# A two-part FFT and channel-mix kernel: engine order from a model in the program, and its PSUM as four bank pairs that any stage may take

## The chip, the core and the metric

The kernel runs on one core of a Trainium2 chip. The time is the device time in microseconds (us). The kernel before comes in two kinds: 802 to 806 us, with a mean granted clock of 0.932 to 0.938 where it is on record, and 810 to 816 us, mostly with 0.914 to 0.926 (four with 0.96). Its profiled execution took 815.3 us, so it is one of the slower kind, and a difference from its profile is up to 10 us larger than one from the faster kind. Runs of it over 1.5% above the fastest of their comparison (two near 815.5, and one at 2218.91) count as slow and are left out of the ratios. TensorE is the matmul engine (PE in the profile; PEld is its weight load), VectorE is DVE, ScalarE is ACT, GpSimd is POOL, and SP issues most DMAs.

## The reference

`x` is 8 batches of 3072 tokens by 256 channels. Cut to what matters:

```python
X = np.fft.rfft(x, axis=1)                     # along the tokens
Yr = Xr @ w_r - Xi @ w_i + b_r                 # complex mix of the channels
Yi = Xr @ w_i + Xi @ w_r + b_i
Y  = sign(Y) * maximum(abs(Y) - 0.01, 0)       # soft shrink of both parts
y  = np.fft.irfft(Y, n=3072, axis=1)
# channel mix: y_prev is y shifted by one token
xk = mu_k * y + (1 - mu_k) * y_prev
xr = mu_r * y + (1 - mu_r) * y_prev
k  = np.maximum(xk @ w_k, 0.0)                 # 256 -> 1024
v  = k * k @ w_v                               # 1024 -> 256
out = sigmoid(xr @ w_r) * v
```

## The kernel before

The transform of 3072 points is split into 96 x 32, so each batch passes through five kinds of units:

- **first**: 96-point transform, result A to SBUF (the on-chip memory), then to HBM (the chip's main memory) and back in another layout (A2);
- **middle**: second transform (XT), mix with the complex weights, the bias and the shrink (Y), and a first inverse step (V), which again goes to HBM and back;
- **last**: 96-point inverse transform (YT);
- **k, r, v**: the token part, in six tiles of 512 tokens per batch.

All matmuls of both kernels write to PSUM tiles. Their pools come to 4096 fp32 columns a kernel, counted here as 8 banks of 512. Before, these are bound to purposes: two single banks for transforms, two pairs for k, two single banks for r and v. In the start, before any token, transforms may use all of them.

```python
psF = ctx.enter_context(tc.tile_pool(name="psF", bufs=2, space=bass.MemoryType.PSUM))
psK = ctx.enter_context(tc.tile_pool(name="psK", bufs=2, space=bass.MemoryType.PSUM))
psV = ctx.enter_context(tc.tile_pool(name="psV", bufs=2, space=bass.MemoryType.PSUM))
# ...
def mix(u):
    ps = ps_fft()
    xt = XT.pop(u)
    for i in range(2):
        o = ps[:, 256 * i:256 * i + 256]
        g = 2 * u + i
        nc.tensor.matmul(o, bsel[:, 1 if g == 0 else 0, :], bb, start=True, stop=False)   # bias: 2 rows
        for w, z0, z00 in ((wr, 64, 128), (wi, 0, 0)):
            for c in range(NCD):
                # ...
                nc.tensor.matmul(o, lhs, w[:, c, :], start=False,
                                 stop=(w is wi and c == NCD - 1))
    r1 = r1_pool.tile([128, 512], BF16, name="r1")
    nc.scalar.activation(r1, ps, AF.Relu, bias=neglam, scale=1.0)
    # ... shrink on VectorE
# ... in last(b):
                eng = "act" if state["early"] and c else "dve"
                copy(eng, yt[:, c, :, half, 4 + 4 * qd:8 + 4 * qd, :],
                     ps[:, 0:384].rearrange("p (n h s) -> p h n s", n=4, h=3))
# ... the order in which the program is written:
        run(first(0))
        run(first(1))
        run(middle(0))
        run(last(0))
        state["early"] = False
        for b in range(B):
            # ... parts: middle(b + 1), first(b + 2), last(b + 1)
            merge(tokens(b), chain(*parts), 6 * 7.7, max(total, 1.0))
```

A scheduler then decides each engine's order from this program order and from what is free.

## Time and profile before

| | kernel before |
|---|---|
| median of the first runs | 805.62 us (804.62 to 813.5) |
| span of the profiled run | 813.5 us |
| TensorE busy | 694.5 us, 85% |
| VectorE, ScalarE busy | 540.5 us, 449.0 us |
| first token matmul | 117.3 us |
| from there to the last v matmul of the seventh batch | 629.2 us |
| from there to the last v matmul of the eighth | 61.3 us |
| from there to the end | 5.7 us |

The span runs from the first to the last instruction. The last four rows are read from the start times of the token matmuls in TensorE's timeline, and add up to it. I call them start, seven batches, last batch and tail. "Busy" counts an engine once while instructions overlap. Idle of TensorE, by who ended it (columns: total us, times, longest):

```profile
PE psK L386 <- DVE xk L374: 14.6, 24, 1.3
PE psF L265 <- DMA A<-Adr: 14.2, 1, 14.2
PE psF L341 <- DVE YT L226: 13.4, 34, 0.8
```

VectorE stands in two of the three: it copies the last transform and makes xk.

### The profile page before, as it was taken

What the parts mean: (1) busy time and instruction counts of PE and PEld (TensorE: products, weight loads), DVE (VectorE), ACT (ScalarE), POOL (GpSimd) and SP (SyncE); (2) the same over time, 40 slices, a digit from 0 to 9 for tenths busy, and PEclk for the clock granted to TensorE, in tenths of its full rate; (3) what the DMA queues carried; (4) which work ended last, traced back from release to release, by engine and by line L of the source; (5) the groups of instructions that cost most, each with busy time, mean ns of one, the idle gap of its engine ahead of it and who ended that gap; (6) DMA issues with size and microseconds to landing.
All of it is one profiled execution on the core that took longest, in us unless ns stands there. A gap on an engine that the chain in (4) does not pass through costs nothing.

```text
span 813.5 us, 12796 instructions
## 1 busy us (share of the span) xinstructions
PE 694.5 (85%) x4839; PEld 441.1 (54%) x4889; DVE 540.5 (66%) x1050; ACT 449.0 (55%) x661; POOL 24.7 (3%) x54
## 2 busy tenths in 40 slices
PE   2439659998999978998799978999799987998897
PEld 1125346665466635665366644666366653766565
DVE  6413249757966396765867587764967577775993
ACT  2324238683765735673566836675456736563463
POOL 5200000000000000000000000000000000000000
PEclk9655559999999989999899999999999999999799
DMA  9991131259222961347422881247413661135122
GB/s 162 233 223 41 52 79 26 67 144 258 52 52 72 234 162 27 91 114 205 110 65 66 214 201 27 64 100 226 110 47 85 193 144 27 52 95 139 27 78 78
DMA packets 75534, 90.38 MB, mean 111 GB/s; under 512 B 8912, under 2 KB 59856, under 8 KB 75472
## 3 DMA queue, kind: packets, MB, share of 16 engines
q1 hardware_dynamic: 69696, 75.53, 34.3%
q0 software_dynamic: 5776, 14.03, 9.8%
q8 instruction: 38, 0.62, 0.3%
q14 instruction: 24, 0.20, 0.1%
HBM read 53.22 MB, written 50.33 MB: 127 GB/s over the span
## 4 chain that ended last, share of the span: by engine, by line
PE 57%; DVE 17%; DMA 10%; ACT 7%; issue 3%; SPq 2%; another core or an unknown queue 0%; ACTq 0%; DVEq 0%
PE psV L419 14%; PE psK L386 12%; PE psF L292 11%; DVE YT L226 5%; PE psF L288 4%; DMA out_dram<-o 3%; PE psV L404 3%; ACT rl L390 3%; DVE k L395 3%; DVE xk L374 3%; PE psF L239 3%; PE psF L274 2%; DMA V<-Vdr 2%; PE psF L303 2%; PE psV L292 2%
## 5 line engine op out<-in xcount | busy, mean ns | idle before, releaser
L390 ACT ACTIVATE rl<-psK 128x1024 bf16<-128x1024 f32 x192 | 192.7, 1025 | 134.8 <-PE psK L386 129.7
L386 PE MATMUL psK<-xk,wk 128*128 128x512 bf16 x718 | 201.9, 398 | 23.7 <-DVE xk L374 14.6
L419 PE MATMUL psV<-wv,k 128*128 128x256 bf16 x1536 | 206.9, 273 | 1.4 <-ACT rg L408 1.2
L395 DVE TENSOR_TENSOR k<-rl 128x1024 bf16<-128x1024 bf16 x192 | 129.1, 687 | 73.5 <-ACT rl L390 73.5
L419 PEld LDWEIGHTS <-k 128*128 128x128 bf16 x1536 | 147.6, 98 | 35.1 <-issue 3.5
L386 PEld LDWEIGHTS <-wk 128*128 128x128 bf16 x768 | 76.2, 101 | 105.3 <-issue 37.0
L295 ACT ACTIVATE r<-psF,neglam 128x512 bf16<-128x512 f32 x86 | 59.2, 688 | 82.8 <-PE psF L292 82.4
L226 DVE CAST YT<-psF 128x384 bf16<-128x384 f32 x115 | 58.9, 552 | 37.8 <-PE psF L341 37.6
L292 PEld LDWEIGHTS <-XT 128*128 128x128 bf16 x768 | 62.2, 101 | 38.5 <-issue 14.2
L424 DVE TENSOR_TENSOR o<-psV,rg 128x512 f32<-128x512 f32 x96 | 65.5, 686 | 26.3 <-PE psV L419 24.0
L297 DVE SCALAR_TENSOR_TENSOR Y<-psF,r 128x512 bf16<-128x512 f32 x86 | 59.0, 686 | 33.5 <-ACT r L295 33.3
L224 ACT ACTIVATE XT<-psF 128x512 bf16<-128x512 f32 (+1 forms) x93 | 52.8, 581 | 40.6 <-PE psF L274 22.2
L408 ACT ACTIVATE rg<-psV 128x512 bf16<-128x512 f32 x96 | 56.4, 597 | 30.9 <-PE psV L404 30.4
L374 DVE SCALAR_TENSOR_TENSOR xk<-diff,muk,YT 128x512 bf16<-128x512 bf16 x96 | 68.5, 745 | 2.3 <-PE psK L386 1.8
L374 DVE SCALAR_TENSOR_TENSOR xr<-diff,mur,YT 128x512 bf16<-128x512 bf16 x96 | 67.8, 745 | 1.0 <-PE psV L404 0.7
L292 PE MATMUL psF<-wr,XT 128*128 128x256 bf16 x344 | 68.3, 281 | 0.0
L341 PE MATMUL psF<-FI,V 96*128 96x96 f16 x468 | 42.5, 219 | 29.4 <-DVE YT L226 13.4
L292 PE MATMUL psF<-wi,XT 128*128 128x256 bf16 x344 | 66.7, 276 | 0.0
L404 PE MATMUL psV<-wrm,xr 128*128 128x256 bf16 x384 | 58.7, 275 | 8.8 <-DVE o L424 7.0
L341 PEld LDWEIGHTS <-V 96*128 96x128 bf16 x512 | 35.4, 108 | 45.5 <-issue 29.1
L224 ACT ACTIVATE A<-psF 96x512 bf16<-96x512 f32 x101 | 55.3, 603 | 3.0 <-DMA Adr<-A 2.1
L288 PE MATMUL psF<-bb,bsel 2*128 2x256 bf16 x172 | 47.9, 279 | 5.1 <-ACT XT L224 3.9
(115 smaller groups left out, 522.9 us busy)
## 6 DMA issues: line engine op xcount, KB each, us to landing
out_dram<-o SPq DMA_DIRECT2D x192, 128.0 KB, 2.2
xs<-in_x_dram POOLq DMA_DIRECT2D x32, 384.0 KB, 8.6
Adr<-A SPq DMA_DIRECT2D x32, 384.0 KB, 8.0
A<-Adr SPq DMA_DIRECT2D x32, 384.0 KB, 6.4
Vdr<-V SPq DMA_DIRECT2D x192, 64.0 KB, 1.8
V<-Vdr SPq DMA_DIRECT2D x32, 384.0 KB, 7.0
wk<-in_moe_w_k_dram POOLq DMA_DIRECT2D x1, 512.0 KB, 9.1
wv<-in_moe_w_v_dram POOLq DMA_DIRECT2D x1, 512.0 KB, 8.7
```

What stands on the lines that cost most here:

```text
L224: nc.scalar.activation(out, in_, AF.Copy, bias=0.0, scale=1.0)
L226: nc.vector.tensor_copy(out=out, in_=in_)
L288: nc.tensor.matmul(o, bsel[:, 1 if g == 0 else 0, :], bb, start=True, stop=False)
L292: nc.tensor.matmul(o, lhs, w[:, c, :], start=False, stop=(w is wi and c == NCD - 1))
L341: nc.tensor.matmul(ps[:, 96 * i:96 * i + 96], V2[b, n2 // 8][:, n2 % 8, 128 * c:128 * c + 128], FI, start=True, stop=True)
L374: nc.vector.scalar_tensor_tensor(out=m[:, c, :], in0=diff[:, c, :], scalar=mu[:, c:c + 1], in1=yp[:, c, :], op0=ALU.mult, op1=ALU.add)
L386: nc.tensor.matmul(ps[:, 512 * f:512 * f + 512], wk[:, c, 128 * ff:128 * ff + 128], xk[:, c, :], start=(c == 0), stop=(c == NCD - 1))
L390: nc.scalar.activation(rl, ps, AF.Relu, bias=0.0, scale=1.0)
L395: nc.vector.tensor_tensor(out=K2[t][:, 2 * i:2 * i + 2, :].rearrange("p f n -> p (f n)"), in0=rl, in1=rl, op=ALU.mult)
L404: nc.tensor.matmul(ps[:, 256 * i:256 * i + 256], xr[:, c, 128 * q:128 * q + 128], wrm[:, c, :], start=(c == 0), stop=(c == NCD - 1))
L419: nc.tensor.matmul(ps[:, 256 * i:256 * i + 256], K2[t][:, ff, 128 * q:128 * q + 128], wv[:, ff, :], start=(ff == 0), stop=(ff == NCF - 1))
L424: nc.vector.tensor_tensor(out=o[:, 2 * p:2 * p + 2, :].rearrange("p q d -> p (q d)"), in0=ps, in1=RG.pop((t, p)), op=ALU.mult)
```

## The change

The intent: keep TensorE fed all the time. The program no longer leaves the order to the scheduler. It simulates the engines while it is being written out: it picks, of six streams of units, the ready one that is due first, gives it whichever bank pair comes free first, lets the engine that would end sooner do each copy, and writes the instructions out in that order. Units are two banks wide. The bias is padded to 128 rows. Loads at the start are reordered. The diff, cut to its core:

```diff
+    ctx.enter_context(tc.manual_schedule())
-    psF = ctx.enter_context(tc.tile_pool(name="psF", bufs=2, space=bass.MemoryType.PSUM))
-    psK = ctx.enter_context(tc.tile_pool(name="psK", bufs=2, space=bass.MemoryType.PSUM))
-    psV = ctx.enter_context(tc.tile_pool(name="psV", bufs=2, space=bass.MemoryType.PSUM))
+    psum = ctx.enter_context(tc.tile_pool(name="psum", bufs=1, space=bass.MemoryType.PSUM))
+    banks = psum.tile([128, 4, 1024], FP32, name="banks")
 ... pools: XT 4 to 3, r1 3 to 2, Y 4 to 3, V 2 to 3, V2 5 to 4, rg 5 to 3 (some of twice the size)
-    bb = const.tile([2, D], BF16, name="bb")
+    bb = const.tile([128, 2, D], BF16, name="bb")
+    nc.vector.memset(bb, 0.0)
 ...
+    def run_on(eng, ready, us):
+        free[eng] = max(ready, free[eng]) + us
+        return free[eng] + 0.1
+    def cheaper(ready, act_us, dve_us):
+        a, d = max(ready, free["act"]) + act_us, max(ready, free["dve"]) + dve_us
+        return "act" if a <= d else "dve"
+    def take():
+        f, i = min((f, i) for i, f in enumerate(pair_free) if f is not None)
+        pair_free[i] = None
+        return banks[:, i, :], i
 ... each stage rewritten as units with a due time, a TensorE time and a list of needs
+                if u or half:
+                    nc.tensor.matmul(ps[:, base:base + 512], bsel[:, 0, :], bb.rearrange("p a d -> p (a d)"),
+                                     start=True, stop=False)
 ... after A2 of batch 0 has been asked for:
+                        nc.gpsimd.tensor_copy(out=junk, in_=A2[0][:, 0, 0:1])
+                        load_big()
+                        for n in range(4):
+                            load_x(1, n)
 ...
+    P = 74.0
+    START = 60.0
+        fb += first(b, 0.0, 1.0) if b == 0 else first(b, *((45.0, 52.0) if b == 1 else (s - 0.9 * P, s - 0.1 * P)))
+        fa += middle(b, 20.0, 44.0) if b == 0 else middle(b, s, s + 0.5 * P)
+        fc += last(b, 55.0, 60.0) if b == 0 else last(b, s + 0.75 * P, s + 0.95 * P)
 ...
+    while any(n < len(s) for n, s in zip(place, streams)):
+        flush(t)
 ...     of the streams' next units that are ready, issue the one due first
```

## The prediction

> **What bounds the kernel now.** I read the page's summary first, then busy time by stretches of the run, then the chain of waits around one slow stretch, then TensorE's timeline instruction by instruction.
>
> ```profile
> PE 694.5 (85%) x4839; PEld 441.1 (54%) x4889; DVE 540.5 (66%) x1050; ACT 449.0 (55%) x661; POOL 24.7 (3%) x54
> ...
> PEclk9655559999999989999899999999999999999799
> ```
>
> TensorE looks busy for 85% of the span, but matmuls overlap, so this isn't time at full rate. The clock row shows about half speed from 40 to 130 us. I therefore count streaming time. In the TensorE timeline ten back-to-back 256-column matmuls take 1.25 us with the last at 0.27, so one needs (1.25 - 0.27)/9 = 0.109 us. A 512-column one needs 0.215, a 128-column one 0.056 and a 96-column one 0.043 (same method). Per batch of the eight: k 96 x 0.215 = 20.7; v 192 x 0.109 = 20.9; r 48 x 0.109 = 5.2; together 46.9 for the token part. Middle: second transform 2.7, bias 24 x 0.109 = 2.6, mix 96 x 0.109 = 10.5, back 24 x 0.109 = 2.6, sum 18.4. First 16 x 0.215 = 3.4; last 64 x 0.043 = 2.7. In all 71.4 us per batch. The boundary between batches (the wait for V) recurs at 271, 363, 456, 548, 640 and 733 us: a period of 92.4 us. So 21 us per period are not streaming.
>
> Where they are lost, by stretches (columns: stretch, its length, busy us and count of each engine, clock, DMA share, GB/s):
>
> ```profile
> 37.00:53.00 16.00, 1.12 (x3) 0.29 (x3) 2.57 (x4) 2.15 (x4) 0.51 (x1) 0.50 1.12 258
> 53.00:98.00 45.00, 41.73 (x192) 21.98 (x190) 14.30 (x30) 18.09 (x31) 0.00 (x0) 0.50 0.28 63
> 98.00:108.00 10.00, 0.00 (x0) 0.00 (x0) 0.00 (x0) 0.00 (x0) 0.00 (x0) 0.50 0.67 176
> ...
> 283.00:315.00 32.00, 23.66 (x153) 12.26 (x156) 25.67 (x56) 13.27 (x16) 0.00 (x0) 0.89 0.45 121
> 315.00:350.00 35.00, 33.67 (x268) 22.89 (x268) 25.37 (x46) 21.55 (x35) 0.00 (x0) 1.00 0.29 76
> ```
>
> First loss: the stretch 283 to 315, where the last transform meets the first tokens of the next batch. Adding up the streaming time of the matmuls that start in it gives 17.6 of 32 us: 14 us lost. The chain of waits there is VectorE alone:
>
> ```profile
> 287.00 3.40 DVE YT L226 x7
> 290.40 0.60 DVE diff L369
> 291.00 0.47 DVE YT L226
> 291.47 1.33 DVE xk L374 x2
> ```
>
> All the copies of the last transform go to VectorE, while ScalarE is at 13.27 of 32 us. Second loss: the bias matmuls, which use 2 of 128 rows. TensorE's timeline:
>
> ```profile
> 333.25 0.38 PE L292 MATMUL psF<-wi,XT 128*128 128x256 bf16 x2
> 333.56 0.28 PE L288 MATMUL psF<-bb,bsel 2*128 2x256 bf16 x1
> 333.77 0.39 PE L292 MATMUL psF<-wr,XT 128*128 128x256 bf16 x2
> ```
>
> Two wi matmuls need 0.22 from 333.25, so the bias could start at 333.47. It starts 0.09 late, and what follows starts 0.21 later instead of 0.11. One bias matmul costs about 0.20 us beyond its own streaming; 24 per batch are 4.8 us. That leaves 21 - 14 - 4.8 = about 2 us per period for all else. Third loss: the start. The first token matmul runs at 117.3 us.
>
> [...] VectorE takes 0.552 for 384 columns and 0.688 for 512, so 1.06 ns a column and 0.14 fixed; ScalarE takes 0.598 for 512 and 1.025 for 1024, so 0.17 fixed. [...] Here TensorE is 41.73 of 45 us busy from 53 to 98 and stays at 0.50, so I can't count on a release at a given point.
>
> **The change part by part.**
> 1. Bias rows padded to 128 (zeros) and, but for the first pair of each batch, one 512-column matmul for two of 256. Streaming stays 2.6 us per batch; the switching goes: -4.8 us per batch, on the path wherever TensorE is the bound. Seven batches after the start: -34.
> 2. Two-bank units. For VectorE, 96 gatings and 96 shrinks of 0.69 become 48 + 48 of an estimated 0.144 + 1024 x 0.00106 = 1.23, which saves 96 x 0.14 = 13 us. ScalarE: 96 mix relus and 96 gates become 48 + 48, saving 96 x 0.17 = 16. Mostly beside TensorE; worth something only in the boundary.
> 3. Copies chosen by who would end first. From the built order of instructions, ScalarE gets 49 of 64 A copies, 51 of 64 YT, 33 of 48 V and 38 of 48 wide XT. ScalarE's sum: 192 x 1.0 + 48 x 1.03 + 48 x 1.1 + 120 x 1.03 + 51 x 0.85 = 462. VectorE's: squares 132, xk and xr 136, diff 33, gating and shrink 118, copies 66, negations and pads 27 = 512. Per batch about 58 and 64 against 71.4 of TensorE: no new bound, but not much slack (80 to 90%).
> 4. Emission in the order of the model, units chosen by readiness, any of four bank pairs. Before, the last transform's 16 units had two one-bank buffers and ran back to back. Now it is due at 75 to 95% of the previous period, interleaved with tokens, and V is asked for half a period earlier. I expect 4 of the 14 us to remain, plus 2 for stalls of an order fixed in advance.
> Period: 71.4 + 4 + 2 = 77.4 us.
> 5. The start. x of batch 0 alone loads first; batch 1's x and the three large weights wait until A2 has arrived; batch 1's first transform follows the middle. Before, DMA was full from 0 to 53 us and A2 (issued at 37.0) landed at 52.9. Now 1.57 MB of x and 0.26 of wr and wi at the measured 161 GB/s are in at about 13 us; A stores of 7 to 8 us end near 24, and A2 [...] lands near 32. The middle took 45 us at half clock; without the switching (24 x 0.2[...]) and with wider units I take 33. Then 10 for the round trip of V and 3 for the last units: tokens from about 78 us, against 117.
>
> Sum: 78 + 7 x 77.4 + last batch. Tokens alone stream 46.9; before, the last stretch took 60 us, 51 of them TensorE busy, with TensorE waiting on VectorE. I take 50. Gating and storing at the end: about 4. 78 + 542 + 50 + 4 = 674, taken as 670: the last two batches have no first transform, which takes off up to 2 x 3.4.
>
> **The rivals.**
> A. TensorE becomes almost continuous and the start gets the full clock. For it: after the bias has gone, only about 2 us per period of other loss were left, and ready work is chosen from six streams. Period 74.5, tokens at 70: 70 + 521 + 49 + 4 = 644.
> B. A fixed order that does not fit. Engines now run in a sequence derived from constants; where a DMA or a wait comes later than assumed, an engine stands before an instruction whose data isn't there while later ones are ready. A mix or v unit holds a bank pair for about 5 us (2.2 or 3.5 of matmuls plus 1.2 to 2.4 of reading), so two of them leave two pairs. Evidence: V took 12.1 us to arrive on the chain at 271 us, more than the 7 us that the diff assumes. Against: the read is now asked for well ahead. Period 84, tokens at 85: 85 + 588 + 52 + 4 = 729.
> C. VectorE becomes the bound. At 64 of 77 us it isn't on average, but squares, token mixing and shrink come in bursts. Period 80 to 82: about 700.
> D. Slower or unchanged: needs a period near 92 again. Only a wrong dependency across the shared bank tile would do that. The built waits of TensorE name single later points of ScalarE and VectorE and do not follow every instruction, so I think it unlikely.
>
> **Range and chances.** Half weight on the main sum, a quarter each side of it; B at its full size is a tail. Predicted 670 us, 636 to 712 eight times in ten. Being within 2% would need more than 110 us to go wrong: faster 0.95, within 2% 0.03, slower 0.02.
>
> **What would show it.** Step 1: no idle before bias weight loads, where the waits before had 43.3 us in 176 cases. Step 3: VectorE near 512 us busy, ScalarE near 462. Step 4: the wait for V off the chain, periods of 75 to 80 us, no stretch of 30 us with half of TensorE's streaming. Step 5: first token matmul before 85 us. I am wrong if the period exceeds 84, if the start stays over 90 us, or if waits on bank pairs or of VectorE lead the chain throughout.

In step 5 two terms go: how the arrival of A2 was counted, and what the delays around the two-row matmuls were taken to be at half clock. The 32 and the 33 us there still count them, so the sum is as recorded: 78 + 542 + 50 + 4 = 674, taken as 670. Without the two, A2 (1.57 MB at the 230 GB/s of 20 to 40 us, so 7 us) lands at 24 + 7 = 31, and the first middle takes 45 - 24 x 0.2 = 40.2 less what the wider units save. "The switching" is the 0.20 us that a bias matmul costs beyond its own streaming. The clock is at half from 27.4 to 119.6 us of the trace, and the DMA share from 0 to 53 us is 1.01.

## The result

The changed kernel takes 667.56 us (median of 4 runs, 664.56 to 670.45); the kernel before took 809.56 in the same comparison. The ratio is 0.8243 (95% interval 0.816 to 0.8326). A ratio is the mean time of one kernel's fast runs over that of the other's of the same rounds, so it is not quite the ratio of the two medians.

| | before | after | difference |
|---|---|---|---|
| start | 117.3 | 87.3 | -30.0 |
| seven batches | 629.2 | 524.4 | -104.8 |
| last batch | 61.3 | 44.8 | -16.5 |
| tail | 5.7 | 6.3 | +0.6 |
| span | 813.5 | 662.8 | -150.7 |

The spans differ by more than the medians (142.0 us), because the profiled execution of the kernel before is one of its slower kind and that of the changed kernel is the fastest of its four. The last batch of the kernel before begins at 746.5 us and still holds matmuls of the last transform until 760.4 us; in the changed kernel they are over before it begins. So not all of the 16.5 us there is a gain of the token part.

The page of the changed kernel, same lines as in the prediction:

```profile
PE 593.6 (90%) x4722; PEld 435.5 (66%) x4801; DVE 483.8 (73%) x732; ACT 443.5 (67%) x469; POOL 25.2 (4%) x57
...
PEclk9689579999999999999999999999999999999999
```

TensorE has lost 94 to 101 us of busy time although it streams almost the same columns (593.6 us here with 79 matmul records missing, 600.2 in the control with none missing): a part was half clock in the start (27.4 to 119.6 us before, 23.1 to 36.7 and 64.0 to 84.5 now), a part the delay around the two-row matmuls (96 ns before one and 101 ns after it, the medians at full clock in the kernel before). How much each was isn't worked out here. After the start the clock stays high: its mean from 87 to 662 us is 0.99, and it is at half only from 91.3 to 98.2 and from 313.2 to 316.6. The dips of the kernel before at each boundary of batches, 3.4 to 10.2 us each, have gone.

By stretches:

```profile
32.00:56.00 24.00, 20.87 (x176) 16.69 (x180) 14.36 (x17) 12.41 (x13) 5.19 (x9) 0.90 0.91 173
56.00:87.00 31.00, 14.78 (x100) 9.29 (x99) 12.15 (x17) 13.62 (x17) 4.04 (x8) 0.67 0.99 238
...
247.00:323.00 76.00, 72.11 (x576) 53.01 (x585) 58.56 (x86) 52.08 (x56) 2.03 (x4) 0.98 0.59 143
```

The first line is the first middle stage: 24 us, where the kernel before needed 45 at half clock. The second is the round trip of V: TensorE is idle half of it, and the DMA share is 0.99. The third is one ordinary period of 76 us: TensorE 72 us busy, VectorE 58.6, ScalarE 52.1. After the start no stretch of 30 us streams for less than 23.8 us (added up matmul by matmul in the control's trace).

The bias in TensorE's timeline:

```profile
49.75 0.60 PE L418 MATMUL banks<-Y,GI 128*128 128x256 bf16 x4
50.19 0.38 PE L383 MATMUL banks<-bb,bsel 128*128 128x512 bf16 x1
50.40 0.38 PE L394 MATMUL banks<-wr,XT 128*128 128x256 bf16 x2
```

Four matmuls of 0.109 from 49.75 end at 50.19, where the bias starts; it streams 512 columns in 0.21 and the next starts at 50.40. Nothing is lost on either side any more.

What TensorE waits for now:

```profile
PE banks L344 <- DMA A<-Adr: 23.5, 5, 12.4
PE banks L287 <- ACT A L234: 11.7, 1, 11.7
PE banks L287 <- DMA xs<-in_x_dram: 7.0, 2, 6.0
PE banks L489 <- DMA V<-Vdr: 3.6, 4, 1.6
```

Waits for VectorE have left the head of this list. In their place stands the DMA of A2 (the first line): once 12.4 us in the start, and then (23.5 - 12.4)/4 = 2.8 us on average before the middle of a batch can begin. The chain of waits shows how the two transfers follow each other ahead of one of these middles:

```profile
217.17 8.52 DMA Adr<-A
227.27 8.81 DMA A<-Adr
```

Store, wait, load: from 217.2 to 236.1 us is 18.9 us, where the model in the program counts 5 + 7.

### The profile page after: what moved, and what is told of

It is laid out like the page before. It is cut to its first block, busy times and chain, and to the rows that moved or that the text cites. A ratio compares the mean times of both kernels' runs of the same rounds, so it can differ in the third digit from the quotient of the medians.

```text
span 662.8 us, 12033 instructions
## 1 busy us (share of the span) xinstructions
PE 593.6 (90%) x4722; PEld 435.5 (66%) x4801; DVE 483.8 (73%) x732; ACT 443.5 (67%) x469; POOL 25.2 (4%) x57
## 3 DMA queue, kind: packets, MB, share of 16 engines
q0 software_dynamic: 5840, 14.03, 12.5%
## 4 chain that ended last, share of the span: by engine, by line
PE 66%; DMA 17%; ACT 6%; DVE 5%; issue 3%; SPq 1%; POOL 0%; DVEq 0%; ACTq 0%; POOLq 0%
PE banks L617 22%; PE banks L575 19%; PE banks L394 11%; DMA Adr<-A 7%; DMA A<-Adr 6%; PE banks L600 4%; ACT rl L581 3%; PE banks L361 3%; PE banks L418 2%; PE banks L383 2%; ACT A L234 2%; PE banks L287 2%; DMA Vdr<-V 1%; DVE V L236 1%; PE banks L489 1%
## 5 line engine op out<-in xcount | busy, mean ns | idle before, releaser
L581 ACT ACTIVATE rl<-banks 128x1024 bf16<-128x1024 f32 x192 | 195.0, 1029 | 86.1 <-PE banks L575 73.2
L575 PE MATMUL banks<-xk,wk 128*128 128x512 bf16 x706 | 191.1, 383 | 4.0 <-DVE xk L553 1.4
L617 PE MATMUL banks<-wv,k 128*128 128x256 bf16 x1536 | 184.5, 274 | 0.4 <-DVE k L587 0.3
L402 ACT ACTIVATE r<-banks,neglam 128x1024 bf16<-128x1024 f32 x48 | 53.4, 1113 | 40.6 <-PE banks L394 39.4
L406 DVE SCALAR_TENSOR_TENSOR Y<-banks,r 128x1024 bf16<-128x1024 f32 x48 | 58.5, 1222 | 28.1 <-ACT r L402 28.0
L394 PE MATMUL banks<-wr,XT 128*128 128x256 bf16 x384 | 73.8, 274 | 0.9
L394 PE MATMUL banks<-wi,XT 128*128 128x256 bf16 x384 | 73.8, 274 | 0.0
L624 DVE TENSOR_TENSOR o<-banks,rg 128x1024 f32<-128x1024 f32 x48 | 58.5, 1218 | 7.7 <-PE banks L617 7.7
L234 ACT ACTIVATE XT<-banks 128x1024 bf16<-128x1024 f32 (+2 forms) x39 | 37.8, 970 | 35.4 <-PE banks L361 23.5
L234 ACT ACTIVATE A<-banks 96x1024 bf16<-96x1024 f32 x49 | 49.2, 1020 | 17.6 <-DMA Adr<-A 12.0
L600 PE MATMUL banks<-wrm,xr 128*128 128x256 bf16 x384 | 49.8, 272 | 3.5 <-ACT rl L581 2.2
L600 PEld LDWEIGHTS <-xr 128*128 128x128 bf16 x384 | 37.1, 97 | 14.1 <-issue 3.8
```

The lines of the kernel that those rows point to most:

```text
L234: nc.scalar.activation(out, in_, AF.Copy, bias=0.0, scale=1.0)
L394: nc.tensor.matmul(o, lhs, w[:, c, :], start=False, stop=(w is wi and c == NCD - 1 and (i == 1 or not (u or half))))
L406: nc.vector.scalar_tensor_tensor(out=y, in0=ps, scalar=LAM, in1=r1, op0=ALU.add, op1=ALU.min)
L575: nc.tensor.matmul(ps[:, 512 * f:512 * f + 512], wk[:, c, 128 * ff:128 * ff + 128], xk[:, c, :], start=(c == 0), stop=(c == NCD - 1))
L581: nc.scalar.activation(rl, ps, AF.Relu, bias=0.0, scale=1.0)
L600: nc.tensor.matmul(ps[:, 256 * q:256 * q + 256], xr[:, c, 128 * q:128 * q + 128], wrm[:, c, :], start=(c == 0), stop=(c == NCD - 1))
```

## The experiments

Twelve kernels ran, all with correct results. They ran in four rounds, each on another chip: the control, two-row bias, halves and fixed engines; then single pairs, scheduler's order, early loads and the padded old kernel; then the earlier first transform, both mends and three parts undone; then two and two. The control ran in the first round alone. The kernel before had medians of 812.23 to 813.89 in the four, so a difference of 2 us between rounds says nothing. "Start", "seven batches" and so on are those of the profiled run.

### The changed kernel again (control)

> The changed kernel unchanged, as the control for the runs beside it. Both theories: 664 to 671 us, ratio to the kernel before 0.82 to 0.83, first token matmul near 87 us, period of the middle batches near 76 us.

667.83 us (666.72 to 668.91), ratio 0.823. Start 90.1, seven batches 523.9, last 44.8. This is the number that the others are compared with; the start moves by some 3 us from run to run.

### Bias back to two rows

```diff
-                    nc.tensor.matmul(ps[:, base:base + 512], bsel[:, 0, :], bb.rearrange("p a d -> p (a d)"),
+                    nc.tensor.matmul(ps[:, base:base + 512], bsel[0:2, 0, :], bb[0:2].rearrange("p a d -> p (a d)"),
-                        nc.tensor.matmul(o, bsel[:, 1 - i, :], bb[:, 0, :], start=True, stop=False)
+                        nc.tensor.matmul(o, bsel[0:2, 1 - i, :], bb[0:2, 0, :], start=True, stop=False)
```

> The changed kernel with the bias rows cut back to 2 of 128 (still one 512-column matmul where the change has one). 13 bias matmuls a batch remain 2-row. Theory 1 (each change between a 2-row and a 128-row matmul costs TensorE 0.1 us on each side, and TensorE is the bound): 8 x 13 x 0.20 = +21 us, 685 to 692 us, and the idle before bias weight loads comes back (about 0.2 us in some 100 cases). Rival (TensorE has slack that takes it up): under +6 us. Besides: if the 2-row matmuls were what held the clock at a half in the first middle stage of the kernel before, the stretch from 32 to 56 us stays at half clock here and the first token matmul moves from 87 us to about 97; if not, it stays within 3 us of 87.

683.67 us (679.89 to 687.43), ratio 0.8425: +16 us. In the profiled run, the slowest of the four, the seven batches took 543.2 (+19) and the start 91.4 (+1). The weight loads of the bias wait again:

```profile
PEld L383 <- issue: 21.8, 69, 0.4
PEld L394 <- issue: 20.4, 88, 0.3
```

The first line is the bias, the second the mix weights right after it, which in the changed kernel waited 0.8 us in all.

From start to start in the trace, the median delay is 95 ns before a 2-row matmul and 101 ns after it, the same for 512 columns as for 256. So theory 1 holds: 0.2 us per bias matmul, on TensorE's path, though the median lies 1 us under its range. The second question got the answer no: the recorded clock was full from 35.4 us to the end of that stage, much as in the control (from 36.6), and its mean over 32 to 56 us is 1.00 (0.90 in the changed kernel), so 13 two-row matmuls did not hold the clock down here. In the changed kernel, then, the padding is not what gives the start its clock.

### The kernel before with the bias padded, nothing else

```diff
-    bb = const.tile([2, D], BF16, name="bb")
+    bb = const.tile([128, D], BF16, name="bb")
+    nc.vector.memset(bb, 0.0)
 ... bsel likewise; its two rows are written as before
```

> The kernel before with nothing but the bias rows padded to 128 with zeros (still two 256-column matmuls). Theory 1 (0.20 us saved per bias matmul, 192 of them, where TensorE is the bound): ratio to the kernel before 0.94 to 0.97, that is -25 to -45 us, the idle of 43 us before bias weight loads gone, and perhaps more if the first middle stage then gets the full clock (another -10 to -20). Rival (the time saved turns into waits for VectorE and for banks): ratio over 0.98.

769.29 us against 813.89, ratio 0.9496: -44 us by the medians, and about -35 against the faster kind of the kernel before (802.39 to 804.6 in this round). Against the profiled execution, one of the slower kind, it falls in two parts. Seven batches went from 629.2 to 603.4 (-25.8), and the idle of 43.3 us before the bias weight loads has gone. The start went from 117.3 to 97.6 (-19.7), nearly all of it in the first middle stage. About 6 us of that are the delays around the two-row matmuls: at half clock their medians in the kernel before were 140 and 109 ns, and 24 x 0.25 = 6.0. The rest goes with the clock:

```profile
53.00:98.00 45.00, 29.02 (x266) 24.46 (x267) 20.89 (x53) 22.08 (x42) 0.00 (x0) 0.75 0.46 111
```

In the kernel before this stretch has a clock of 0.50 and TensorE is busy 41.73 us. Here the recorded clock is full from 58.5 us and returns to half only at 79.0, after the stage is over. Nothing but the padding differs, and the four runs with it agree (767.86 to 769.55), so in these profiles the half clock went with the 24 two-row matmuls of that stage. It need not do so in every execution: the faster runs of the kernel before (802 to 806 us) have the same 24 and a higher mean clock, and none of them was profiled. With the run before this: 24 went with the half clock, 13 did not, though the width and order of the units differ between the two as well. What decides it isn't shown.

### Two-bank readings cut into one-bank halves

```diff
-                    nc.scalar.activation(r1, ps, AF.Relu, bias=neglam, scale=1.0)
+                    for z in (slice(0, 512), slice(512, 1024)):
+                        nc.scalar.activation(r1[:, z], ps[:, z], AF.Relu, bias=neglam, scale=1.0)
 ... likewise the shrink, the gate, the gating, and the two halves of each copy
```

> The changed kernel, same bank pairs and nearly the same order, but every reading of a bank pair is done in two one-bank halves (the relu and shrink of the mix, the gate, the gating, and the copies; the relu of k stays whole, as in both kernels). About 267 more ScalarE instructions and 156 more VectorE ones. Theory 1 (wide readings save ScalarE and VectorE time that is mostly off TensorE's path): ScalarE busy +30 to +40 us, VectorE +15 to +20, time +0 to +10 us. Rival (VectorE or ScalarE is the bound): +20 us or more.

662.36 us (660.18 to 664.64), ratio 0.8163: 5 us faster than the control, whose four runs lie between 666.72 and 668.91. ScalarE's busy time rose from 443.8 to 466.6 (+23) and VectorE's from 484.2 to 494.1 (+10), less than expected, because instructions that follow each other overlap (their durations added up rose by 55 and 23). In the profiled run 2 us of the gain lie in the start, 2 in the seven batches and 0.5 in the tail. So wide readings are no gain in this kernel; they cost about 0.8%. Neither theory said that. A reading of one bank is shorter (0.598 us against 1.025 for two on ScalarE in the kernel before), so the first bank of a halved unit could come free sooner for the next matmuls; whether it does, and whether that is the cause, no run here isolates.

### Engines of the copies fixed

```diff
-    def copy(ready, out, in_, act_us, dve_us):
-        eng = cheaper(ready, act_us, dve_us)
+    def copy(ready, out, in_, act_us, dve_us, eng="act"):
 ... YT copies get "dve", V copies "dve" if u % 2 else "act"
```

> The changed kernel with each copy's engine fixed as in the steady part of the kernel before: A and XT on ScalarE, V by turns, YT on VectorE. VectorE gets about 51 more YT copies of 0.95 us and loses some 25 others. Theory 1 (the boundary between batches was lost to VectorE's copies of the last transform, and the free choice of engine is what mended it): +10 to +25 us, with VectorE waits of the last transform's matmuls back on the chain. Rival (interleaving the last transform with tokens mends it by itself, whichever engine copies): under +5 us.

682.21 us (681.22 to 684.11), ratio 0.841: +14 us, of which 6 in the start (96.2) and 10 in the seven batches (533.7). The size fits theory 1, but its sign of recognition failed: no wait of the last transform for VectorE is among TensorE's larger waits; the DMAs of A2 (26.1 us) and V (14.1 us) lead. The free choice of engine is worth 14 us; that it is worth them at the boundary isn't shown. Ten us in seven batches are 1.4 of the 14 us per period that the prediction put down to these copies.

### Order left to the scheduler

```diff
-    ctx.enter_context(tc.manual_schedule())
```

> The changed kernel without the manual schedule: the same program, pairs and engine choices, but each engine's order is left to the scheduler that orders the kernel before. Theory 1 (the order made by the model is a large part of the gain): +25 us or more, with waits of TensorE between batches. Rival (bank pairs, wide units, bias and the engine choice make the gain, and the program's order is good enough for any scheduler): within 10 us of the changed kernel.

691.27 us (690.13 to 694.84), ratio 0.8544: +23 us, 19 of them in the seven batches (542.9), 6 in the start. That is just under theory 1's 25 and far from the rival's 10. Its sign, waits of TensorE between batches, is weak: nine waits for V, 9.9 us in all. The order that the model gives is worth about 23 us. The program is still written in the model's sequence here, so this is the value of holding to it exactly, not of the model as a whole.

### Three parts undone at once

The last, the fixed engines and the two-row bias together.

> The changed kernel with three parts undone at once: bias rows of 2, engines of the copies fixed, and the order left to the scheduler. Alone these cost 16, 14 and 24 us. If they are independent: 668 + 54 = 722 us, and the remaining 90 us up to the kernel before lie in what is left: the units taken by readiness from six streams into freely shared bank pairs, and the start. If they cover for one another (each lets the others' lost time show): 740 us or more.

730.4 us (729.72 to 733.07), ratio 0.9029. Alone the three cost 16, 14 and 23, together 53; at once they cost 63. That is 10 us more than the sum, and halfway between the two expectations (722 and 740), so they cover for one another a little. What remains to the kernel before, 82 us by the medians (812.23 and 730.4), lies in parts that none of the three touches. No wait of the last transform for VectorE leads TensorE's list here either; the DMA of V does (23.2 us).

### One pair for all transforms

```diff
+    PAIRS = {0: (0, 1), 1: (2,), 2: (3,), 3: (3,), 4: (3,), 5: (0, 1, 2, 3)}
-        f, i = min((f, i) for i, f in enumerate(pair_free) if f is not None)
+        f, i = min((pair_free[i], i) for i in PAIRS[s] if pair_free[i] is not None)
 ... stream 0 is k and r, 1 is v, 2 middle, 3 first, 4 last, 5 the tables; slot_ready(s) likewise
```

> The changed kernel with the four bank pairs bound to stages: two for k and r, one for v, one for all transforms and the mix (nearest to the kernel before in two-bank units); the order is made anew by the same model. Theory 1 (free use of pairs is part of the gain: with one pair a transform's matmuls wait for the reading of the one before): a mix unit holds its pair for some 5 us and a transform for some 1.7, so a batch's middle, first and last need 6 x 5 + 28 x 1.7 = 78 us of one pair, which is over the period of 76: period 80 to 95, time +30 to +120 us. Rival (pairs have slack; only the order matters): under +10 us.

893.14 us (890.72 to 897.39), ratio 1.1034: slower than the kernel before. Periods were about 102 us. TensorE stands before its own stage's single pair:

```profile
PE banks L289 <- ACT A L234: 49.0, 44, 1.2
PE banks L491 <- ACT YT L234: 38.6, 43, 0.9
```

Each of these is a matmul that waits for the reading of the unit before it, some 0.9 to 1.1 us at a time. The clock suffers too: its mean is 0.837 against 0.961 in the control, with 34 us at half clock in a period (209.6 to 243.7 us, and again from 312.0). How much of the 225 us is the clock and how much the waits isn't separated. The kernel before had two single banks for the same units. With the due times left as they were, units two banks wide in a single pair lose the whole gain and more.

### Two pairs for tokens, two for the rest

```diff
+    PAIRS = {0: (0, 1), 1: (0, 1), 2: (2, 3), 3: (2, 3), 4: (2, 3), 5: (0, 1, 2, 3)}
```

> The changed kernel with the bank pairs bound more mildly than in the run with single pairs: two for the token stages (k, r, v), two for the transforms and the mix; order made anew by the same model. By holding times a token part needs 24 x 2.1 + 6 x 2.1 + 6 x 4.9 = 92 us of two pairs per batch, 46 of a period of 76, and the rest 78 us of two pairs, 39 of 76. Theory 1 (free sharing itself is a large part of the gain, since each side at times needs three pairs or more): +15 to +60 us, and the last batch, tokens alone on two pairs, goes from 44.8 us to 50 or more. Rival (only a stage left with a single pair is slow, as that first run was; two and two are as good as four shared): under +8 us, last batch within 2 us of 44.8.

720.14 us (714.23 to 724.18), ratio 0.8861: +52 us. Start 101.5, seven batches 553.7, last batch 55.6. The last batch is the clean case, tokens with nothing else beside them. TensorE there, with two pairs:

```profile
685.62 1.03 PE L577 MATMUL banks<-xk,wk 128*128 128x512 bf16 x4
687.76 1.03 PE L602 MATMUL banks<-wrm,xr 128*128 128x256 bf16 x8 [1.11 <-ACT rl L583]
688.63 1.03 PE L577 MATMUL banks<-xk,wk 128*128 128x512 bf16 x4
689.90 1.91 PE L619 MATMUL banks<-wv,k 128*128 128x256 bf16 x16 [0.25 <-ACT rg L607]
```

My reading is that a v unit sits on one pair, so k and r take turns on the other and wait for ScalarE. TensorE is idle for 8.3 of 56 us in this last batch. With four shared pairs the same stretch has no wait of TensorE, and its last batch 0.8 us of idle in 45:

```profile
628.34 1.04 PE L600 MATMUL banks<-wrm,xr 128*128 128x256 bf16 x8
629.21 1.89 PE L575 MATMUL banks<-xk,wk 128*128 128x512 bf16 x8
630.94 1.91 PE L617 MATMUL banks<-wv,k 128*128 128x256 bf16 x16
```

Holding times alone (46 and 39 of 76 us by the estimate) would have let two and two pass. So the average isn't what counts; that it is the moment at which a third pair is wanted fits the lines above. The due times in the program were not tuned anew for this binding, so 52 us is an upper figure for the value of sharing.

### Loads of the start as before

```diff
-                        nc.gpsimd.tensor_copy(out=junk, in_=A2[0][:, 0, 0:1])
-                        load_big()
-                        for n in range(4):
-                            load_x(1, n)
 ... and up at the head:
+    load_x(1, 0)
+    load_big()
+    for q in range(1, 4):
+        load_x(1, q)
```

> The changed kernel with x of batch 1 and the three large weights asked for at once, as in the kernel before, rather than after A2 of batch 0. Theory 1 (at the start the DMA engines are the bound, so what loads first decides): A2 lands 8 to 14 us later than at 32 us, the first middle stage starts at 40 to 46, but less is left to load afterwards, so the first token matmul is only 0 to 8 us later: 667 to 676 us. Rival (the late loads are what made the start fast): +10 to +15 us.

665.84 us (664.68 to 666.42), ratio 0.822: within 2 us of the control. The first middle starts at 43.0 instead of 32.1 and the first token matmul at 97.2 instead of 90.1, but the seven batches then take 515.9 instead of 523.9. What the late loads win in the start, 7 us, is paid back after it. Theory 1 holds for the start; the total came out 1 us under its range.

### The first transform due sooner

```diff
-        fb += first(b, 0.0, 1.0) if b == 0 else first(b, *((45.0, 52.0) if b == 1 else (s - 0.9 * P, s - 0.1 * P)))
+        fb += first(b, 0.0, 1.0) if b == 0 else first(b, *((45.0, 52.0) if b == 1 else (s - 1.1 * P, s - 0.3 * P)))
```

> The changed kernel with the first transform of each later batch due 0.2 period sooner (1.1 to 0.3 periods ahead in place of 0.9 to 0.1), nothing else. In the changed kernel the middle's first matmul waits for the DMA of A2 five or six times, 24 us in total, about 12 of it at the start and some 2.4 at each of five later batches. Theory 1 (this new wait is on TensorE's path): the later waits go, period 76 to 73.5, -8 to -13 us, 655 to 660. Rival (the wait only covers time that VectorE or the bank pairs would take anyway): within 4 us of the changed kernel's 668.

658.44 us (657.74 to 659.39), ratio 0.813: -9 us. Seven batches 516.0 (-8). TensorE's wait for A2:

```profile
PE banks L344 <- DMA A<-Adr: 15.7, 3, 12.5
```

Three waits are left, one of them the 12.5 us of the start. So the new wait was on the path, and one constant removes it.

### Both mends together

> The one-bank readings (which came out 5 us faster than the wide ones) and the earlier first transform together. If the two are independent: 662 less 8 to 13, so 649 to 654 us. If what the halves gained was the same wait in another form (a bank of a pair comes free sooner, so the first transform's stores start sooner): no better than the better of the two alone.

654.73 us (653.09 to 655.9), ratio 0.8082: 13 us better than the changed kernel, and the best of all. The two gains (5 and 9) nearly add; the sum would have been 653.

## Why the prediction was right, and where its steps were not

The total was right (670 predicted, 667.56 measured), but partly by luck: errors of both signs cancelled. The recorded sum is 78 + 542 + 50 + 4 = 674, against a span of 662.8:

| term | predicted | measured | error |
|---|---|---|---|
| start | 78 | 87.3 | too small by 9.3 |
| seven batches and last batch | 592 | 569.2 | too large by 22.8 |
| tail | 4 | 6.3 | too small by 2.3 |

**Step 1, the bias: the delay right, size over in the batches.** The 0.2 us per two-row matmul was confirmed at 0.095 + 0.101. Padding alone gave -25.8 in the seven batches of the old kernel, less than the -34 of the step. It also gave -19.7 in the start there, which the step didn't count: "I can't count on a release at a given point". In the changed kernel undoing it moves the start by 1 us only. For the first middle the prediction took more than the 0.2 us; at half clock it measured 0.25.

**Step 2, wide units: failed as a saving.** The step expected 13 and 16 us less work. Undoing it, together with the halves of the copies, which the step hadn't counted, added 10 and 23 us of busy time, but the time fell by 5. "Mostly beside TensorE" was right; the sign of what was left was not.

**Step 3, copies and engine loads: right, sizes over.** VectorE was busy 483.8 us against 512 predicted, ScalarE 443.5 against 462; adding durations counts overlap twice (added up, they are 525.9 and 472.6). The copies fell to the engines just as forecast. No new bound came. The free choice is worth 14 us.

**Step 4, the period: mechanism right, size over.** 77.4 predicted; the end of v recurs every 75.7 us on average from the first to the sixth batch. The boundary has dissolved, as expected. What the step blamed for it, VectorE's copies of the last transform, is not what the runs confirm: with those copies back on VectorE the waits stayed away and only 1.4 us per period returned. That the interleaving dissolved it is the likely reading; no run isolates it. (Added up again from the trace, the stretch from 283 to 315 streams for 17.0 us, not 17.6; some matmul records are missing.) The step left 6 us per batch for what could go wrong; much of what did was one wait that it didn't name, the DMA of A2, 2.8 us at a time. Of the 22.8 us too large, some 8 come from those five periods; the largest part, some 11 us, is the seventh batch, beside which no first transform is left and which took 66.7 us; the last batch, put down as 50, took 44.8. The prediction allowed 4 us for this when it rounded 674 to 670.

**Step 5, the start: failed in both halves.** The first middle took 24 us, not 33; the clock was full from 36.7 us on. The way from its end to the first token took 31 us, not 13. The timeline shows why (start, length, what):

```profile
49.27 10.92 SPq L431 DMA_DIRECT2D Vdr<-V  x16
60.30 1.44 SPq L298 DMA_DIRECT2D Adr<-A  x3
71.16 1.95 SPq L442 DMA_DIRECT2D V<-Vdr  x4
76.43 0.50 PE L489 MATMUL banks<-FI,V 96*128 96x96 f16 x4 [1.60 <-DMA V<-Vdr]
79.94 4.34 PE L489 MATMUL banks<-FI,V 96*128 96x96 f16 x52 [0.37 <-DMA V<-Vdr]
87.29 0.38 PE L575 MATMUL banks<-xk,wk 128*128 128x512 bf16 x1 [1.11 <-DVE xk L553]
```

V's stores were issued until 60.2 us, but had all landed only at 71.0, when the queue could ask for V again: the last took 11.4 us to land, where the median V store of the first 110 us took 3.9. V was back at about 80 us. Meanwhile A of batch 1 went out and more of x came in, and from 56 to 87 us the DMA engines were 99% busy at 238 GB/s. The step treated V's round trip as if it had the DMA engines to itself. The kernel before had needed 21 us for the same way (96.7 to 117.3). And the load order, on which the step rested, is worth 7 us of start but nothing in the total (the run with early loads, where this way takes the same 31 us). Of the prediction's own signs the one for this step failed: the first token came after 85 us, and in the control the start, 90.1, just passed the 90 at which the prediction called itself wrong.

**The rivals.** B named the right danger, a DMA later than the model assumes, but for V; it came for A2 and in the start, and after the start it cost the 9 us that the earlier first transform wins back, where B at full size would have cost 55. C (VectorE as the bound) did not come: waits for VectorE no longer lead TensorE's list, and the run with halves has more VectorE work and less time. A was nearest for the period.

What the parts are worth, as far as the runs show: bias 16 us when undone, and 35 to 44 when done alone; order 23; choice of engine 14; load order about 0; wide readings -5; sharing of the pairs up to 52. These sum to 100 of the 146 us. The rest, some 40 to 50 us, is by elimination the units' free interleaving over six streams together with what the parts do to one another; no single run isolates it.

## What to carry to other kernels

Share PSUM by time, not by purpose: binding the same four bank pairs two and two cost 8%, although the holding times said there was room, and one to all transforms cost 34%. Look for matmuls with few rows in a stream of full ones, since here each cost about 0.2 us beyond its streaming, and padding with zeros took 4 to 5% off the old kernel. When an order is fixed in advance from assumed transfer times, read the trace for the first wait on a DMA and move that work's due time: one constant gave another 1.4%.
